# Mixing stage of a fused three-part kernel: where the next batch's value splits and the weight-rounding steps are issued

## The chip, the cores and the metric

The kernel runs on one core of one Trainium2 chip. The metric is the device time of one execution in microseconds (us). A core has TensorE (PE, matrix products), VectorE (DVE), ScalarE (ACT), GpSimd (POOL) and the queues that issue transfers, above all that of SyncE (SP). Each engine works through its own list of instructions in order; engines wait for each other through semaphores. On-chip data lies in SBUF (128 partitions), matrix products in the eight banks of PSUM.

## The reference

Three parts run one after the other. The change lies in the second, and in the preparation of the third's weights that runs beside it.

```python
# 1: delta-rule attention over (4, 8 heads, 768, 48), giving x of shape (4, 768, 384)
# 2:
h = gelu(x @ w_in)                       # (4, 768, 1024)
u, v = h[..., :512], h[..., 512:]
v_n = (v - mean(v)) / sqrt(var(v) + 1e-06) * g_ln
v_s = einsum('ts,bsd->btd', w_sg, v_n) + b_sg[None, :, None]     # the mixing over the 768 positions
x = x + (u * v_s) @ w_out                # gate, projection, addition
# 3:
k = relu(xk @ w_k); v = k * k @ w_v; r = sigmoid(xr @ w_r); out = r * v    # xk, xr: x mixed with its shift
```

All is float32. A product is made of three products of rounded parts: each operand is split into a high part `hi`, rounded to the format that PE multiplies fast, and a low part `lo = x - hi`, and `hi*hi + hi*lo + lo*hi` is summed (`mm3`, and `mix_mm` for the mixing).

## The kernel before, in words

The attention and the input projection come first; they leave the values v and the gates u in device memory (`vn_d`, `u_d`). The mixing follows, and after it the third part (ffn), in which PE is never without work for long.

**Halves.** The mixing runs over eight halves, `halves[k]` for k = 0 to 7, that is batch b = k // 2 and output half t = k % 2 (384 of the 768 positions). Below, h0 to h7. A half has four row blocks d (128 of the 512 channels). `mix(b, t, d)` multiplies the six chunks c of the batch's values with the half's mixing weights (18 matmuls into one PSUM bank), then gates on DVE: scale and bias out of PSUM (L897), multiplication with u (L899), and the split into `gh` (ACT, L108) and `gl` (DVE, L111). `project(b, t)` multiplies the four gated blocks with w_out (three groups of 12 matmuls, L139), each group followed by an addition into `xT` on DVE (L912 before, L911 in the changed kernel). For t = 0, `begin` first opens all four row blocks, so that PE does 48 matmuls (60 in h0) chunk by chunk. The projection of h(k-1) is put behind `begin` in an even half, behind the third row block in an odd one. PE's order is written out by hand (`manual_schedule`); the other engines' lists are made by a scheduler from the order of the program and its estimates.

**Values.** `load_v(b, c)` brings chunk c of batch b from device memory into `vst` (three buffers, L818, on SP's queue) and splits it into `vh` (ACT, L108) and `vl` (L111, 128x512) in a ring of nine; each of its chunks is read by both halves of its batch. The low part is made on GpSimd, for c = 0 and 3 on DVE. For the next batch three of the loads are issued ahead of the even half's last row block (`VF`), and all six splits behind the second row block of the odd half (`VD`).

**Weight roundings.** Beside all this the weights of the ffn are rounded and split by jobs (`narrow`): a load (L148, SP), six steps on DVE (L157, L159, L161, L163, L165, L167), an addition on POOL (L168), a rounding on ACT (L108), a subtraction on POOL (L111, `na<-na,raw`), and two stores (L196, SP). Steps on w_k are 128x256, on w_r and w_v 128x384. Two jobs are open at a time. `side(n)` issues the next n steps of the jobs; before the change it stands at three places: one step between the gate multiplication and the split, `SD` = 2 behind the split, and one behind each addition of a projection.

Of the kernel before, what the change touches and what calls it, by code (L numbers as in the profile page):

```python
# [16 lines left out]
B, H, S, D = 4, 8, 768, 48  # L17
# [32 lines left out]
NGL = 3  # L50
NNA = 2
PD = 2
SD = 2
CS = (5, 4)
VF = (0, 3)
VD = 1

E_LO_F = 2.0 ** -15
E_HI_F = 122879.9921875
# [15 lines left out]
def fused_kernel(  # L75
# [741 lines left out]
        vsts[b, c] = vr.tile([P, HF], F32, name="vst", bufs=3)  # L817
        nc.sync.dma_start(out=vsts[b, c], in_=vn_d[b, c])  # L818

    def load_v(b, c):  # L820
        if (b, c) not in vsts:
            fetch_v(b, c)
        to_ring(b, c, vsts.pop((b, c)))

    def to_ring(b, c, vst):
        vh = vr.tile([P, HF], F32R, name="vh")
        vl = vr.tile([P, HF], F32R, name="vl")
        split(A, G if c % 3 else V, vst, vh, vl)
        ring[b, c] = (vh, vl)

    ahead = [lambda i=i: load_ws(0, i) for i in range(6)]
# [55 lines left out]
    def mix(b, t, d):  # L887
        sl = slice(t * DM, t * DM + DM)
        pt, c0 = begun.pop(d, (None, 0))
        if pt is None:  # L890
            pt = ps.tile([P, HF], F32, name="ms")
        for c in range(c0, 6):
            mix_mm(pt, b, t, d, c)
        if d == 0:
            gs[b, t] = [mp.tile([P, 4, DM], F32R, name=x) for x in ("gh", "gl")]
        w = mp.tile([P, DM], F32, name="w")
        V.scalar_tensor_tensor(w, pt[:, :DM], g_sb[:, d:d + 1], b_sb[:, sl],  # L897
                               op0=ALU.mult, op1=ALU.add)
        V.tensor_tensor(w, w, us[b, t][:, d], op=ALU.mult)  # L899
        side(1)  # L900
        split(A, V, w, gs[b, t][0][:, d], gs[b, t][1][:, d])
        side(SD)

    def project(b, t):
        gh, gl = gs.pop((b, t))
        for f in range(3):
            pt = ps.tile([P, HF], F32, name="ms")
            fs = slice(f * P, f * P + P)
            mm3(pt[:, :DM], [((wo[0][:, c, fs], wo[1][:, c, fs]), (gh[:, c], gl[:, c]))
                             for c in range(4)])  # L910
            xs = xT[:, b, f, 1 + t * DM:1 + t * DM + DM]  # L911
            V.tensor_tensor(xs, xs, pt[:, :DM], op=ALU.add)  # L912
            side(1)

    load_u(0, 0)
    load_u(0, 1)
# [10 lines left out]
    for k, (b, t) in enumerate(halves):  # L927
# [6 lines left out]
        for d in range(4):  # L934
            if (t, d) == VF and b + 1 < B:
                for c in range(3):
                    fetch_v(b + 1, c)
            mix(b, t, d)
            if d == (PD if k < 7 else 3) and t:
                project(*halves[k - 1])  # L940
            if t == 1 and d == VD and b + 1 < B:
                for c in range(6):
                    load_v(b + 1, c)
        if k == 7:
            side(999)
        if k == 6:
# [123 lines left out]
```

## Time and profile before

| what | value |
|---|---|
| median of 3 runs | 811.81 us (810.57 to 814.44) |
| profiled execution, its own time | 811.44 us |
| its span in the trace | 809.7 us |
| granted TensorE clock, mean | 0.97 |
| PE busy | 747.1 us (92%) |
| DVE busy | 583.3 us (72%) |
| ACT busy | 344.3 us (43%) |
| POOL busy | 186.9 us (23%) |
| first matmul of the mixing to the end of its last projections | about 396 to 561 us |

How to read it: the shares are averages over three stages. The mixing is a fifth of the span; what an edit in it is worth is read from the places where PE waits there. Rows of a timeline give the start in us, the duration, the engine, the line of the program, what is written and read, and, in brackets, the idle time before the row and what ended it. "PEclk" is the granted clock, 1.00 being 2.4 GHz and 0.50 being 1.2 GHz.

### The profile page before, as it was taken

How to read it: one execution, taken by the hardware profiler on the slowest of the kernel's cores; microseconds unless marked ns; L12 is line 12 of the kernel's file. 1: busy time of each engine (PE TensorE's matmuls, PEld its weight loads, DVE VectorE, ACT ScalarE, POOL GpSimd, SP SyncE). 2: the span in 40 equal slices, each digit the busy share in tenths (PEclk: the TensorE clock that was granted, in tenths of full speed). 3: DMA queues.
4: the chain of work that ended last, by engine and by line, in shares of the span. 5: the costliest groups of instructions: out<-in, count | busy, mean ns of one | idle time of the engine just before them, and what ended most of it. 6: DMA issues, size and time to landing. Idle time of an engine off the chain costs nothing.

```text
span 809.7 us, 23901 instructions
## 1 busy us (share of the span) xinstructions
PE 747.1 (92%) x10206; PEld 656.5 (81%) x10206; DVE 583.3 (72%) x1253; ACT 344.3 (43%) x681; POOL 186.9 (23%) x197
## 2 busy tenths in 40 slices
PE   3368999999999998978989899899999999999998
PEld 3335667768778676767889799799999999999998
DVE  7989999689699698234779896988945655653442
ACT  2213454465555644634632231316744544542331
POOL 4125342232131323323324453340000000000000
PEclk9978999999999999989999889899999999999999
DMA  8403353354353443437987646449200000000000
GB/s 231 90 27 100 91 118 87 95 155 140 94 150 83 132 121 92 137 99 184 277 266 247 202 128 194 145 127 292 59 30 21 20 20 20 20 21 30 11 20 30
DMA packets 84970, 89.21 MB, mean 110 GB/s; under 512 B 25856, under 2 KB 68992, under 8 KB 84864
## 3 DMA queue, kind: packets, MB, share of 16 engines
q1 hardware_dynamic: 80128, 78.64, 32.8%
q0 software_dynamic: 4736, 9.04, 4.2%
q8 instruction: 80, 1.31, 0.7%
q14 instruction: 26, 0.21, 0.1%
HBM read 56.86 MB, written 26.08 MB: 102 GB/s over the span
## 4 chain that ended last, share of the span: by engine, by line
PE 60%; DVE 18%; DMA 7%; issue 6%; POOL 3%; ACT 2%; SPq 2%; DVEq 0%; POOLq 0%; ACTq 0%
PE ms L139 32%; PE ms L618 5%; PE ms L659 4%; PE rk L432 3%; PE ms L567 3%; PE ms L298 2%; DVE tmp L321 2%; PE ms L884 2%; DMA raw<-in_w_k_dram 2%; PE ms L502 2%; PE rk L468 2%; PE sps L488 2%; PE rk L444 2%; POOL na L168 1%; DVE na L157 1%
## 5 line engine op out<-in xcount | busy, mean ns | idle before, releaser
L168 POOL TENSOR_TENSOR na<-raw,na 128x256 f32<-128x256 f32 (+2 forms) x43 | 40.2, 938 | 149.7 <-DVE raw L167 110.0
L659 PE MATMUL ms<-warm 128*128 128x512 bf16 x222 | 62.1, 405 | 9.0 <-DVE warm L407 9.0
L139 PE MATMUL ms<-wvh,sh 128*128 128x384 f32 x192 | 64.9, 338 | 0.0
L139 PE MATMUL ms<-wvl,sh 128*128 128x384 f32 x192 | 64.9, 338 | 0.0
L139 PE MATMUL ms<-wvh,sl 128*128 128x384 f32 x192 | 64.8, 338 | 0.0
L139 PE MATMUL ms<-xm_hi,wkh 128*128 128x384 f32 x192 | 64.1, 334 | 0.0
L139 PE MATMUL ms<-xm_lo,wkh 128*128 128x384 f32 x192 | 64.1, 334 | 0.0
L139 PE MATMUL ms<-xm_hi,wkl 128*128 128x384 f32 x192 | 64.1, 334 | 0.0
L432 PEld LDWEIGHTS rk<-r,DT 32*32 32x32 f32 x1536 | 36.2, 107 | 28.7 <-DVE r L424 18.5
L111 DVE TENSOR_TENSOR sl<-r,sh 128x384 fp32r<-128x384 f32 x64 | 35.8, 559 | 30.3 <-ACT sh L108 30.3
L454 POOL TENSOR_SCALAR_AFFINE_SELECT SQ<-SQ 64x512 f32<-64x512 f32 x48 | 36.4, 759 | 86.6 <-ACT SQ L453 85.1
L432 PE MATMUL rk<-r,DT 32*32 32x48 f32 x1536 | 42.8, 205 | 13.0 <-DVE r L424 12.7
L424 DVE TENSOR_TENSOR r<-vk,rk 128x384 f32<-128x384 f32 x48 | 26.4, 549 | 38.4 <-PE rk L468 23.9
L108 ACT ACTIVATE sh<-r 128x384 fp32r<-128x384 f32 x64 | 33.6, 525 | 35.9 <-DVE r L990 35.9
L108 ACT ACTIVATE raw<-na 128x256 fp32r<-128x256 f32 (+2 forms) x31 | 13.7, 442 | 80.0 <-POOL na L168 78.1
L1006 DVE TENSOR_TENSOR ob<-th,ms 128x384 f32<-128x384 f32 x24 | 13.3, 553 | 43.3 <-PE ms L139 43.3
L300 PE MATMUL ms<-kT 64*32 64x64 f32 (+1 forms) x896 | 30.6, 225 | 13.9 <-issue 13.9
L618 PE MATMUL ms<-xh,wiu_hi 128*128 128x256 f32 x144 | 43.0, 298 | 0.0
L618 PE MATMUL ms<-xh,wiu_lo 128*128 128x256 f32 x144 | 42.9, 298 | 0.0
L618 PE MATMUL ms<-xl,wiu_hi 128*128 128x256 f32 x144 | 42.3, 294 | 0.6 <-issue 0.6
L990 DVE TENSOR_TENSOR r<-r 128x384 f32<-128x384 f32 x64 | 35.5, 554 | 9.6 <-ACT r L989 9.6
L157 DVE TENSOR_SCALAR na<-raw 128x256 uint32<-128x256 uint32 (+2 forms) x43 | 19.8, 461 | 30.1 <-DMA raw<-in_w_v_dram 7.7
(158 smaller groups left out, 2295.3 us busy)
## 6 DMA issues: line engine op xcount, KB each, us to landing
kT<-in_kt_d_dram SPq DMA_DIRECT2D x12, 512.0 KB, 4.5
u_d<-ug SPq DMA_DIRECT2D x48, 128.0 KB, 2.0
u<-u_d SPq DMA_DIRECT2D x8, 768.0 KB, 5.3
vn_d<-v SPq DMA_DIRECT2D x23, 256.0 KB, 3.9
vst<-vn_d SPq DMA_DIRECT2D x23, 256.0 KB, 3.4
SQ<-in_q_d_dram SPq DMA_DIRECT2D x48, 96.0 KB, 3.6
vk<-in_vk_dram SPq DMA_DIRECT2D x24, 192.0 KB, 3.9
vk<-in_vk_dram SPq DMA_DIRECT2D x12, 384.0 KB, 4.1
```

Of the source, the lines that this page charges most:

```text
L108: A.activation(hi, src, AF.Copy)
L111: eng_lo.tensor_tensor(lo, src, hi.bitcast(F32), op=ALU.subtract)
L139: T.matmul(pt, lhsT=a, rhs=b, start=(i == 0), stop=(i == n - 1))
L157: V.tensor_scalar(a, w_hi, 0x7FFFFFFF, None, op0=ALU.bitwise_and)
L168: G.tensor_tensor(af, f, af, op=ALU.add)
L300: T.matmul(gps[r + 32:r + 64, p, c0:c1], lhsT=t[r:r + 64, u, 32:64], rhs=vw2(t, r, 64, u * C + 32, [(0, (c1 - c0) // 32), (1, 32)]), start ...
L424: V.tensor_tensor(t, vt[s][:, 8 * o:8 * o + 8, :], RQs[o][:, :, 0:D], op=ALU.add)
L432: T.matmul(RQs[o][b0:b0 + 32, p, 0:D], lhsT=DT[b0:b0 + 32, u0 + p, :], rhs=t[b0:b0 + 32, p, :], start=True, stop=True, skip_group_check=True)
L454: G.affine_select(out=pt, in_=pt, pattern=[[0, 8], [1, C]], compare_op=ALU.is_gt, fill=0.0, base=0, channel_multiplier=-1)
L618: T.matmul(vstat["u"][:, 2 * P * d:2 * P * d + 2 * P], lhsT=w[:, c, ds_], rhs=a[:, c].rearrange("p b t -> p (b t)"), start=first, stop=last)
L659: T.matmul(o, lhsT=warm, rhs=vw(warm, 0, [(0, 4), (1, P)]), start=True, stop=True)
L990: V.tensor_tensor(r, r, r, op=ALU.mult)
```

## The change

The constants `SD` and `VD` give way to two tables, `ROW[t][d]` for the steps behind each row block and `ADD[t]` for those behind each addition. The step between the gate multiplication and the split is gone. In an even half one step follows each row block, in an odd half 2, 2, 1 and 8; each addition of the projection of an even half (which runs in an odd half) is followed by 5 steps, each of an odd half's by 2. An even half's calls then issue 10 steps (4, and 3 x 2 in the projection of the odd half before it), an odd half's 28 (13, and 3 x 5); before it was 15 in each (4 x 3, and 3 x 1). The splits of the next batch's values are issued one behind each row block of the odd half (chunks 0 to 2), chunk 3 ahead of the last row block's matmuls and 4 and 5 behind it; each load into `vst` of chunks 3 to 5 follows the split that frees its buffer. All these splits have their low part on GpSimd, none on DVE.

```diff
@@ -50,10 +50,10 @@
 NGL = 3
 NNA = 2
 PD = 2
-SD = 2
+ROW = ((1, 1, 1, 1), (2, 2, 1, 8))
+ADD = (5, 2)
 CS = (5, 4)
 VF = (0, 3)
-VD = 1
 
 E_LO_F = 2.0 ** -15
 E_HI_F = 122879.9921875
@@ -817,15 +817,15 @@
         vsts[b, c] = vr.tile([P, HF], F32, name="vst", bufs=3)
         nc.sync.dma_start(out=vsts[b, c], in_=vn_d[b, c])
 
-    def load_v(b, c):
+    def load_v(b, c, eng=None):
         if (b, c) not in vsts:
             fetch_v(b, c)
-        to_ring(b, c, vsts.pop((b, c)))
-
-    def to_ring(b, c, vst):
+        to_ring(b, c, vsts.pop((b, c)), eng)
+
+    def to_ring(b, c, vst, eng=None):
         vh = vr.tile([P, HF], F32R, name="vh")
         vl = vr.tile([P, HF], F32R, name="vl")
-        split(A, G if c % 3 else V, vst, vh, vl)
+        split(A, eng or (G if c % 3 else V), vst, vh, vl)
         ring[b, c] = (vh, vl)
 
     ahead = [lambda i=i: load_ws(0, i) for i in range(6)]
@@ -897,9 +897,8 @@
         V.scalar_tensor_tensor(w, pt[:, :DM], g_sb[:, d:d + 1], b_sb[:, sl],
                                op0=ALU.mult, op1=ALU.add)
         V.tensor_tensor(w, w, us[b, t][:, d], op=ALU.mult)
-        side(1)
         split(A, V, w, gs[b, t][0][:, d], gs[b, t][1][:, d])
-        side(SD)
+        side(ROW[t][d])
 
     def project(b, t):
         gh, gl = gs.pop((b, t))
@@ -910,7 +909,7 @@
                              for c in range(4)])
             xs = xT[:, b, f, 1 + t * DM:1 + t * DM + DM]
             V.tensor_tensor(xs, xs, pt[:, :DM], op=ALU.add)
-            side(1)
+            side(ADD[t])
 
     load_u(0, 0)
     load_u(0, 1)
@@ -935,12 +934,18 @@
             if (t, d) == VF and b + 1 < B:
                 for c in range(3):
                     fetch_v(b + 1, c)
+            nextv = t and b + 1 < B
+            if nextv and d == 3:
+                load_v(b + 1, 3, G)
             mix(b, t, d)
+            if nextv and d < 3:
+                load_v(b + 1, d, G)
+                fetch_v(b + 1, d + 3)
+            if nextv and d == 3:
+                load_v(b + 1, 4, G)
+                load_v(b + 1, 5, G)
             if d == (PD if k < 7 else 3) and t:
                 project(*halves[k - 1])
-            if t == 1 and d == VD and b + 1 < B:
-                for c in range(6):
-                    load_v(b + 1, c)
         if k == 7:
             side(999)
         if k == 6:
```

What the scheduler makes of it is seen in the order of the instructions. First DVE at the start of the gating, from the last mixing weights' splits (`ws1l`) to the first `gl` of h0; `raw` and `na` belong to one rounding job, a - stands only in the kernel before:

```order
 L111 TENSOR_TENSOR ws1l<-wst,ws1h 128x384 x5
 L897 SCALAR_TENSOR_TENSOR w<-ms,g_sb,b_sb 128x384 x2
-L157 TENSOR_SCALAR na<-raw 128x256
-L159 TENSOR_SCALAR na<-na 128x256
-L161 TENSOR_SCALAR na<-na 128x256
-L163 SCALAR_TENSOR_TENSOR na<-raw,na 128x256
-L165 TENSOR_SCALAR raw<-na 128x256
-L111 TENSOR_TENSOR vl<-vst,vh 128x512
-L167 SCALAR_TENSOR_TENSOR raw<-raw 128x256
 L899 TENSOR_TENSOR w<-w,u 128x384 x2
 L111 TENSOR_TENSOR gl<-w,gh 128x384 x2
```

One whole job and the split of batch 1's chunk 0 no longer stand ahead of the first gate multiplication.

Second, DVE between the last row block of h1 and the first addition of h1's projection. Before, from the last step of a w_k job on, ahead of the last `gl` of h1 (`na_7672` is a w_r job, 384 wide; `na_7246` a w_k job; `vl_7376` the split of a chunk of the next batch's values):

```order
L167 SCALAR_TENSOR_TENSOR raw_7041<-raw_7041 128x256
L157 TENSOR_SCALAR na_7672<-raw_7634 128x384
L111 TENSOR_TENSOR gl_6941<-w_7114,gh_6940 128x384
L159 TENSOR_SCALAR na_7672<-na_7672 128x384
L157 TENSOR_SCALAR na_7246<-raw_7121 128x256
L111 TENSOR_TENSOR vl_7376<-vst_7288,vh_7375 128x512
L159 TENSOR_SCALAR na_7246<-na_7246 128x256
L161 TENSOR_SCALAR na_7672<-na_7672 128x384
L161 TENSOR_SCALAR na_7246<-na_7246 128x256
L163 SCALAR_TENSOR_TENSOR na_7672<-raw_7634,na_7672 128x384
L163 SCALAR_TENSOR_TENSOR na_7246<-raw_7121,na_7246 128x256
```

In the changed kernel, from the last step of a w_r job on (`na_7639` is a second w_r job, `na_7117` and `na_7131` are w_k jobs):

```order
L167 SCALAR_TENSOR_TENSOR raw_7491<-raw_7491 128x384
L111 TENSOR_TENSOR gl_6924<-w_7106,gh_6923 128x384
L159 TENSOR_SCALAR na_7117<-na_7117 128x256
L157 TENSOR_SCALAR na_7639<-raw_7533 128x384
L161 TENSOR_SCALAR na_7117<-na_7117 128x256
L159 TENSOR_SCALAR na_7639<-na_7639 128x384
L163 SCALAR_TENSOR_TENSOR na_7117<-raw_7059,na_7117 128x256
L161 TENSOR_SCALAR na_7639<-na_7639 128x384
L165 TENSOR_SCALAR raw_7059<-na_7117 128x256
L157 TENSOR_SCALAR na_7131<-raw_7115 128x256
L167 SCALAR_TENSOR_TENSOR raw_7059<-raw_7059 128x256
```

Two w_r jobs stand in this stretch where there was one, and the split of a value chunk has left it.

Third, SP from the second three loads of batch 3's values (`vst`) to the w_v load (`raw`) that follows the stores of an earlier w_v job. Before:

```order
L818 DMA vst_7777<-vn_d_67 128x512
L818 DMA vst_7783<-vn_d_67 128x512
L818 DMA vst_7789<-vn_d_67 128x512
L196 DMA wr_dh_6779<-raw_7729 128x384
L196 DMA wr_dl_6780<-na_7823 128x384
L196 DMA wv_dh_6781<-raw_7821 128x384
L196 DMA wv_dl_6782<-na_7903 128x384
L148 DMA raw_7901<-in_w_v_dram 128x768
```

In the changed kernel:

```order
L818 DMA vst_7756<-vn_d_67 128x512
L818 DMA vst_7789<-vn_d_67 128x512
L818 DMA vst_7827<-vn_d_67 128x512
L196 DMA wv_dh_6781<-raw_7700 128x384
L196 DMA wv_dl_6782<-na_7821 128x384
L196 DMA wv_dh_6781<-raw_7819 128x384
L196 DMA wv_dl_6782<-na_7869 128x384
L148 DMA raw_7867<-in_w_v_dram 128x768
```

The stores ahead of the load are those of two w_v jobs now, where one of w_r and one of w_v were; the load still stands behind the three `vst` loads and four stores.

## Rows read from the trace of the kernel before

**Rows 1.** Windows: us; PE, PEld, DVE, ACT, POOL busy (instructions); clock; DMA; GB/s.

```profile
430.00:440.00 10.00, 10.00 (x60) 10.00 (x59) 9.83 (x19) 3.35 (x8) 5.37 (x6) 1.00 0.46 156
...
460.00:470.00 10.00, 8.56 (x20) 5.68 (x21) 9.38 (x24) 3.60 (x8) 2.11 (x4) 0.57 0.60 185
...
500.00:520.00 20.00, 16.66 (x73) 13.90 (x72) 19.15 (x38) 5.15 (x10) 7.42 (x6) 0.83 0.36 126
```

**Rows 2.** Timeline of PE in the mixing: first matmuls behind waits, last ahead of one.

```profile
418.80 0.44 PE L139 MATMUL ms<-gl,wo_hi 128*128 128x384 f32 x1 [0.48 <-DVE gl L111]
...
421.35 0.44 PE L139 MATMUL ms<-gh,wo_hi 128*128 128x384 f32 x1 [1.40 <-ACT gh L108]
...
458.15 0.34 PE L884 MATMUL ms<-ws1h,vl 128*128 128x384 f32 x1
...
460.94 0.44 PE L139 MATMUL ms<-gh,wo_hi 128*128 128x384 f32 x1 [2.45 <-ACT gh L108]
...
486.97 0.44 PE L139 MATMUL ms<-gl,wo_hi 128*128 128x384 f32 x1
...
510.32 0.69 PE L139 MATMUL ms<-gh,wo_hi 128*128 128x384 f32 x1 [1.70 <-ACT gh L108]
```

**Rows 3.** Timeline of DVE: the scale and bias of h2 d0, h3 d3 and h4 d0.

```profile
458.02 0.61 DVE L897 SCALAR_TENSOR_TENSOR w<-ms,g_sb,b_sb 128x384 f32<-128x384 f32 x1
...
482.34 0.61 DVE L897 SCALAR_TENSOR_TENSOR w<-ms,g_sb,b_sb 128x384 f32<-128x384 f32 x1
...
502.40 0.60 DVE L897 SCALAR_TENSOR_TENSOR w<-ms,g_sb,b_sb 128x384 f32<-128x384 f32 x1
```

**Rows 4.** Timeline of DVE: what a step and a value split take.

```profile
413.66 0.29 DVE L159 TENSOR_SCALAR na<-na 128x256 f32<-128x256 f32 x1
...
413.99 0.29 DVE L161 TENSOR_SCALAR na<-na 128x256 uint32<-128x256 uint32 x1
...
432.04 0.69 DVE L111 TENSOR_TENSOR vl<-vst,vh 128x512 fp32r<-128x512 f32 x1
...
467.20 0.29 DVE L165 TENSOR_SCALAR raw<-na 128x256 uint32<-128x256 uint32 x1
...
467.40 0.29 DVE L157 TENSOR_SCALAR na<-raw 128x256 uint32<-128x256 uint32 x1
...
476.00 0.35 DVE L165 TENSOR_SCALAR raw<-na 128x384 uint32<-128x384 uint32 x1
...
476.27 0.35 DVE L157 TENSOR_SCALAR na<-raw 128x384 uint32<-128x384 uint32 x1
```

**Rows 5.** Timelines of POOL and DVE: steps and a split beside POOL splits.

```profile
433.30 2.63 POOL L111 TENSOR_TENSOR vl<-vst,vh 128x512 fp32r<-128x512 f32 x2
...
434.82 1.26 DVE L161 TENSOR_SCALAR na<-na 128x256 uint32<-128x256 uint32 x1
...
481.13 1.28 DVE L111 TENSOR_TENSOR vl<-vst,vh 128x512 fp32r<-128x512 f32 x1
```

**Rows 6.** Timeline of DVE: first gate rows, first additions of the projections of h0, h1.

```profile
416.20 1.53 DVE L899 TENSOR_TENSOR w<-w,u 128x384 f32<-128x384 f32 x2 [0.19 <-DMA u<-u_d]
...
420.19 1.01 DVE L899 TENSOR_TENSOR w<-w,u 128x384 f32<-128x384 f32 x2
...
423.33 2.32 DVE L899 TENSOR_TENSOR w<-w,u 128x384 f32<-128x384 f32 x2
...
427.24 0.55 DVE L912 TENSOR_TENSOR xT<-xT,ms 128x384 f32<-128x384 f32 x1
...
450.97 0.55 DVE L912 TENSOR_TENSOR xT<-xT,ms 128x384 f32<-128x384 f32 x1
```

**Rows 7.** Timelines of POOL, SP and DVE around the w_v load (SPq: the issue).

```profile
491.40 1.03 POOL L168 TENSOR_TENSOR na<-raw,na 128x384 f32<-128x384 f32 x1 [0.89 <-DVE raw L167]
...
494.11 0.32 SPq L196 DMA_DIRECT2D wv_dl<-na  x1
...
497.79 0.36 DVE L157 TENSOR_SCALAR na<-raw 128x384 uint32<-128x384 uint32 x1 [6.00 <-DMA raw<-in_w_v_dram]
```

## The prediction, made before the changed kernel was run

> **What bounds the kernel now.** The windows come first: through the mixing DVE is busy 9 tenths of the time and more [rows 1], while PE loses time in two stretches above all, 460 to 470 (20 matmuls instead of 60, 0.57 of the clock granted) and 500 to 520 (73 instead of 120, 0.83 granted). Then the timeline of PE: from 396 to 561 us PE waits in the projections alone, for the gated blocks `gh` and `gl` [rows 2]. In the projection of h0 it waits 0.48 and 1.40 us; in that of h2 2.45, after which each next block comes in DVE's time; that of h3 starts nearly without a wait (486.97), that of h4 waits 1.70 in one place and goes in DVE's time. Third, the timeline of DVE says why. PE had the row blocks of h2 ready long before, but DVE gets to the first of them, L897, at 458.02 [rows 3], 0.13 us before PE comes to the end of the row blocks ahead of the projection (458.15). DVE works its list in order, and ahead of this row stand rounding steps. So what counts is how many rows stand in DVE's list ahead of three rows: h2 d0 (458.02), h3 d3 (482.34) and h4 d0 (502.40).
>
> **Prices.** Steps of 256 that don't wait for each other follow at 0.20 us (467.20 to 467.40), a step that needs the one ahead at 0.33 (413.66 to 413.99), steps of 384 at 0.27; for a dependent 384 step I add the same 0.13 and estimate 0.40 [rows 4]. A value split on DVE costs 0.60 (432.04, 0.69 with its overlap). A split on POOL takes 1.3 (2.63 for two), and beside it a DVE step took 1.26 instead of 0.29, so 0.97 more; a DVE split 1.28 [rows 5]. I price each POOL split that comes to lie beside steps at 0.97; the bounds are 0 (it lies beside rows out of PSUM or beside a wait) and 1.3 (its whole length).
>
> The Trainium skill, page "SBUF — State Buffer", section "SBUF: two separate sides", has a rule that speaks against this change: GpSimd and certain operations of DVE share a port pair under an exclusive lock, held for the whole instruction by whichever starts first, while the other fully blocks. By it the moved splits and all other POOL rows would cost DVE their whole length, and the time would be that of the slower rival below, 819.6 instead of 815.2; the row at 434.82 agrees in kind, at three quarters of the length.
>
> **Part 1, the start.** A job (six steps), one value split and the POOL rows of both no longer stand ahead of the first gate multiplication. That row waited for the transfer of u (0.19), so the steps themselves gain nothing; but the two L899 took 1.53 there, and an undisturbed pair 1.01; a later pair took 2.32 [rows 6]. Gain in the projection of h0: at least 0.5, at most the 1.88 that PE waits there; I take 0.9. DVE reaches the first addition of that projection (427.24) 0.9 + 0.7 = 1.6 earlier, the 0.7 being about half of the 1.31 that the later pair lost beside POOL splits, which are moved nearby, not removed.
>
> **Part 2, from the first addition of h0's projection (427.24) to that of h1's (450.97), 23.7 us.** Before, DVE has 25 steps of 256, 6 of 384 and 2 value splits there, after it 29, 12 and none, because the odd half now issues 28 steps and not 15. Steps: 4 x 0.20 + 6 x 0.27 = 2.4 if none depends, 4 x 0.33 + 6 x 0.40 = 3.7 if all do; two jobs interleave, so I take 2.8. Splits off DVE: 2 x 0.60 = -1.2. The same two splits beside the steps from POOL: 2 x 0.97 = +1.9. POOL's two rows of one more job, bounded by 0 and 1.3: +0.8. Sum +4.3; less the 1.6 of part 1, the first addition of h1's projection ends 2.7 later, at 450.97 + 0.55 + 2.7 = 454.2. **A new wait** hangs on this. All eight banks are taken there (four of h2, three of h1's projection, one of h3's first block), so the second row block of h3 waits for this addition. PE starts it 36 matmuls ahead of 458.15 [rows 2]; at 60 matmuls in 10 us [rows 1] that is 6.0 us earlier, 452.2, and before the bank was free at 451.5, 0.7 ahead. After, PE is there at 451.3 and waits till 454.2, 2.9 us: PE goes from 0.9 early to 2.0 late.
>
> **Part 3, up to h2 d0.** From that addition to L897 of h2 d0 DVE has 11 steps before and 8 after: -1.0 (3 x 0.33). L897 stands 2.7 - 1.0 = +1.7 late, and then the same number of steps stands between the blocks. So the projection of h2 ends about 1.8 later. This replaces the 2.0 of part 2, it is not added to it: PE arrives later and waits less.
>
> **Part 4, h3 d3.** From L897 of h3 d2 to that of d3 (482.34) there are 10 steps and a split (1.28, stretched) before, 14 steps and no split after, all near 0.40: +1.6 - 1.3; the split now made on POOL beside them +1.0. Together +1.3, so h3 d3 is 3.1 late. Nothing covers it: PE comes to the projection of h3 at 486.97 without idle time to give. That wait, now 1.3, is at once on the path: +3.1.
>
> **Part 5, h4.** DVE stands idle for 6.00 us until 497.79, for a w_v load [rows 7]. The load was issued behind a store at 494.11 that itself needs the POOL addition of 491.40 and the low part after it. In the new order of SP the load still stands behind three `vst` loads and four stores, so the chain moves with DVE: 3 to 4 us, I take 3.5 for L897 of h4 d0, and the rows from there to the last `gl` are as many as before. Queued behind the waiting step on DVE are the additions of h3's projection and then h4's gating.
>
> **Part 6, h5.** 13 steps against 14 and a split, with a POOL split more: -0.4 - 0.6 + 1.0 = 0; the 0.3 left is the split's stretch (1.28 less 0.97). The sum is 3.5 + 0.3 = +3.8, of which the parts are +1.8, +1.3, +0.4 and +0.3. The ffn has no slack and no gain.
>
> **The rivals.** *Faster: the w_v load comes loose.* The changed kernel is some ten steps further ahead in its jobs by h3, so a w_v load goes out earlier. If the load that bounds h4 is among those and lands ahead of 497, DVE's 6.0 idle shrinks to nothing and the projection of h4, which costs (120 - 73) / 120 x 20 = 7.8 us [rows 1], starts on time: 3.1 - 7.8 = -4.7, 806.7. Against it: the load has only two buffers and stands behind the stores in SP's list. *Same: the splits cost nothing.* If POOL's splits fall beside waits or rows out of PSUM, three times 0.97 goes, and the +3.8 becomes +0.9: 812.3. For it: L897 and L912 rows keep 0.55 to 0.61 throughout. *Slower: POOL keeps DVE out for all that it does.* If each added POOL row beside steps takes its whole length from DVE, part 2 pays two splits and the two rows of one more 384 job (1.03 for one at 491.40, [rows 7]): 2.6 + 2.1 = 4.7 instead of 2.7, and part 4 a split and two such rows, 1.3 + 2.1 = 3.4 instead of 1.0, so +4.4: 819.6. It decides from where POOL's rows start in the middle of a run of steps rather than beside L897 or L912. For it: 434.82 and 481.13 were stretched twofold and more. Against it: three quarters is what the row shows, and DVE was 9.83 of 10 us busy and PE without a wait where POOL was already 5.37 busy. *It doesn't do what it says*: the scheduler could put the steps back; the orders show it doesn't.
>
> **How the numbers follow.** The profiled execution took 811.44 (span 809.7 and 1.7 around it), 0.37 under the median. Forecast 811.44 + 3.8 = 815.2. 0.5% of 811.81 is 4.06 us, about what a measurement here can tell from no change: faster means below 807.75, slower above 815.87. The forecast's own range, from part 2's bounds (POOL prices 0 or 1.3, all steps dependent or none), is 812 to 818. Chances: forecast 0.50, of which 0.27 within 0.5% and 0.23 over; splits free 0.18 (within); POOL in full 0.13 (slower); load loose 0.19, of which 0.16 is faster and 0.03 within. Together faster 0.16, same 0.48, slower 0.36. The range 808.5 to 819 leaves out most of the faster case and half of the slower one, some 0.2.
>
> **What would show it.** Right: an idle time of 2 to 3 us ahead of h3's second row block, released by DVE L911; L897 of h2 d0 near 459.7 and of h3 d3 near 485.4; the projection of h3 starting with a wait of about 1.3; DVE idle for a w_v load near 500. Wrong: L911 of h1's projection at or ahead of 451 (steps and splits overpriced), no idle time on DVE around 495 (the load loose), or steps beside POOL rows stretched by more than 1.0 in most places.

## The result, and the profile after

The changed kernel is slower: 825.38 us (822.16 to 827.04, four runs) beside 813.12 us (810.57 to 815.81, four runs) of before, a ratio of 1.0146 (95% interval 1.0098 to 1.0193). In a second comparison on one chip it was 822.99 against 815.98 us, ratio 1.0087 (1.0063 to 1.0112). The forecast was 815.2, the range 808.5 to 819.0: the sign was right, the size too small, the time outside the range.

The first thing to settle is where the profiled execution loses its 14.2 us (span 823.9 against 809.7). The first matmul of the mixing (L884) stands at 396.05 before:

```profile
396.05 0.34 PE L884 MATMUL ms<-ws0h,vh 128*128 128x384 f32 x1
```

The same timeline of PE after: this first matmul, and then the first matmuls behind waits, as in [rows 2]:

```profile
403.12 0.34 PE L884 MATMUL ms<-ws0h,vh 128*128 128x384 f32 x1
...
427.74 0.44 PE L139 MATMUL ms<-gh,wo_hi 128*128 128x384 f32 x1 [1.39 <-ACT gh L108]
...
428.33 0.51 PE L139 MATMUL ms<-gl,wo_hi 128*128 128x384 f32 x1 [0.15 <-DVE gl L111]
...
463.36 0.69 PE L884 MATMUL ms<-ws1h,vh 128*128 128x384 f32 x1 [3.16 <-DVE xT L911]
...
474.14 0.44 PE L139 MATMUL ms<-gh,wo_hi 128*128 128x384 f32 x1 [0.41 <-ACT gh L108]
...
500.36 0.69 PE L139 MATMUL ms<-gl,wo_hi 128*128 128x384 f32 x1 [2.21 <-DVE gl L111]
...
523.95 0.54 PE L139 MATMUL ms<-gh,wo_hi 128*128 128x384 f32 x1 [1.24 <-ACT gh L108]
```

The mixing starts at 403.12, so 7.1 us are lost ahead of it, where PE has the same list in both kernels and the other engines nearly the same one; the granted clock differs there (0.90 before and 0.78 after in the first 100 us). From this matmul to the end it is 420.8 us against 413.7: +7.1, and that is the part which the prediction spoke of. Against the start of the mixing, the blocks end as follows (each is the start of the next block's first matmul):

| end of the projection of | before | after | change that arises there | forecast for it |
|---|---|---|---|---|
| h0 | 31.0 | 31.9 | +0.9 | -0.9 |
| h2 | 77.6 | 81.7 | +3.2 | +2.7 |
| h3 | 95.5 | 103.4 | +3.8 | +1.3 |
| h4 | 123.0 | 130.2 | -0.7 | +0.4 |
| h5 | 142.0 | 149.1 | -0.1 | +0.3 |
| sum | | | +7.1 | +3.8 |

The windows after, with the columns of [rows 1]:

```profile
430.00:440.00 10.00, 10.00 (x54) 10.00 (x53) 9.77 (x21) 3.56 (x7) 3.85 (x4) 0.90 0.79 281
...
440.00:450.00 10.00, 10.00 (x60) 10.00 (x59) 10.00 (x15) 2.51 (x5) 7.14 (x7) 1.00 0.62 195
...
450.00:460.00 10.00, 10.00 (x59) 9.88 (x57) 6.97 (x17) 1.36 (x3) 7.83 (x8) 1.00 0.30 103
...
460.00:470.00 10.00, 6.84 (x24) 6.64 (x23) 8.67 (x20) 1.46 (x3) 4.52 (x6) 0.66 0.74 235
...
500.00:510.00 10.00, 9.64 (x47) 9.64 (x48) 3.60 (x6) 1.16 (x2) 4.69 (x4) 0.83 0.68 228
```

DVE is at its limit from 430 to 450, but from 450 to 460 it is busy only 6.97 of 10 us, while POOL goes up from 3.85 to 7.83. The granted clock is below 1.00 in three of these windows, one of them (430 to 440) a window in which it was 1.00 before [rows 1]. The timeline of DVE after, with the rows that answer to [rows 3, 6, 7]: the first gate multiplication, the first additions of the projections of h0 (432.46) and h1 (462.76), the idle time ahead of the latter, L897 of h2 d0 (468.59) and of h3 d3 (494.71), and the step that waits for the w_v load:

```profile
423.36 1.03 DVE L899 TENSOR_TENSOR w<-w,u 128x384 f32<-128x384 f32 x2 [6.67 <-DMA u<-u_d]
...
432.46 0.54 DVE L911 TENSOR_TENSOR xT<-xT,ms 128x384 f32<-128x384 f32 x1
...
458.75 0.83 DVE L157 TENSOR_SCALAR na<-raw 128x256 uint32<-128x256 uint32 x1 [2.96 <-DMA wk_dl<-na]
...
462.76 0.55 DVE L911 TENSOR_TENSOR xT<-xT,ms 128x384 f32<-128x384 f32 x1
...
468.59 0.61 DVE L897 SCALAR_TENSOR_TENSOR w<-ms,g_sb,b_sb 128x384 f32<-128x384 f32 x1
...
494.71 0.60 DVE L897 SCALAR_TENSOR_TENSOR w<-ms,g_sb,b_sb 128x384 f32<-128x384 f32 x1
...
512.81 0.36 DVE L157 TENSOR_SCALAR na<-raw 128x384 uint32<-128x384 uint32 x1 [9.11 <-DMA raw<-in_w_v_dram]
```

Ahead of h1's first addition there is an idle time of 2.96 us that before does not have there. It ends when a store of a low part (`wk_dl<-na`) lands and frees the buffer `na` for the next step. The timeline of POOL, then of SP, shows where that store came from:

```profile
452.82 2.67 POOL L168 TENSOR_TENSOR na<-raw,na 128x256 f32<-128x256 f32 x1 [1.64 <-DVE raw L167]
...
456.03 0.73 POOL L111 TENSOR_TENSOR na<-na,raw 128x256 fp32r<-128x256 f32 x1 [0.53 <-ACT raw L108]
...
456.79 0.32 SPq L196 DMA_DIRECT2D wk_dl<-na  x1
```

The POOL addition at 452.82 took 2.67 us, the low part ended at 456.76, the store went out at 456.79, the step began at 458.75. POOL was not late with this addition: it had stood idle for 1.64 us ahead of it. The row was long while DVE ran short steps without a pause. Through this chain the bank of h3's second row block came free only at 463.3, and PE waited 3.16 us (463.36), where the prediction had 2.9.

The windows from the first addition of h0's projection to that of h1's, before and then after, part the growth of this stretch into rows and idle time of DVE (third busy time in a line):

```profile
427.24:450.97 23.73, 23.73 (x139) 23.73 (x138) 22.55 (x43) 6.43 (x12) 13.14 (x13) 1.00 0.61 206
...
432.46:462.76 30.30, 27.74 (x160) 27.42 (x158) 26.94 (x51) 7.12 (x14) 20.39 (x18) 1.00 0.55 178
```

Of the 6.6 us more, 4.4 are busy time of DVE and 2.2 idle time (1.18 before, 3.36 after).

### The profile page after: what moved, and what is told of

The parts are those of the page before. It is cut to its first block, busy times and chain, and to the rows that moved or that the text cites. A ratio compares the mean times of both kernels' runs of the same rounds, so it can differ in the third digit from the quotient of the medians.

```text
span 823.9 us, 23901 instructions
## 1 busy us (share of the span) xinstructions
PE 757.9 (92%) x10206; PEld 667.9 (81%) x10206; DVE 581.3 (71%) x1247; ACT 342.7 (42%) x681; POOL 194.6 (24%) x203
## 4 chain that ended last, share of the span: by engine, by line
PE 61%; DVE 18%; DMA 7%; issue 6%; POOL 4%; ACT 2%; SPq 2%; DVEq 0%; POOLq 0%; ACTq 0%
PE ms L139 31%; PE ms L618 5%; PE ms L659 5%; PE ms L567 4%; PE rk L432 4%; PE ms L298 2%; DVE tmp L321 2%; PE ms L884 2%; PE ms L502 2%; POOL na L168 2%; PE sps L488 2%; PE rk L468 2%; PE rk L444 2%; DVE na L157 1%; PE ms L300 1%
## 5 line engine op out<-in xcount | busy, mean ns | idle before, releaser
L432 PE MATMUL rk<-r,DT 32*32 32x48 f32 x1536 | 44.2, 209 | 13.6 <-DVE r L424 13.3
L108 ACT ACTIVATE sh<-r 128x384 fp32r<-128x384 f32 x64 | 33.5, 524 | 35.9 <-DVE r L995 35.9
L157 DVE TENSOR_SCALAR na<-raw 128x256 uint32<-128x256 uint32 (+2 forms) x43 | 21.1, 491 | 34.4 <-DMA wk_dl<-na 10.6
L659 PEld LDWEIGHTS <-warm 128*128 128x128 bf16 x222 | 18.4, 103 | 29.3 <-DVE warm L407 9.6
```

What stands on the lines that cost most here:

```text
L108: A.activation(hi, src, AF.Copy)
L157: V.tensor_scalar(a, w_hi, 0x7FFFFFFF, None, op0=ALU.bitwise_and)
L432: T.matmul(RQs[o][b0:b0 + 32, p, 0:D], lhsT=DT[b0:b0 + 32, u0 + p, :], rhs=t[b0:b0 + 32, p, :], start=True, stop=True, skip_group_check=True)
L659: T.matmul(o, lhsT=warm, rhs=vw(warm, 0, [(0, 4), (1, P)]), start=True, stop=True)
```

## The experiments

All times in this table are worked out from the timelines of PE and DVE of one profile each, against the first matmul of the mixing: where the blocks end, how long h3's projection lasts, the bank wait at h3's second row block (- if under 1 us), the stretch on DVE from the first addition of h0's projection to that of h1's, the landing of the w_v load that ends DVE's idle time ahead of h4, and the rest to the end of the span. The ratio is that of the timed runs.

| kernel | mixing starts | h0 ends | stretch | bank wait | h2 ends | h3 lasts | w_v lands | h4 ends | rest | ratio |
|---|---|---|---|---|---|---|---|---|---|---|
| before | 396.1 | 31.0 | 23.7 | - | 77.6 | 6.5 | 101.7 | 123.0 | 413.7 | 1 |
| before, again | 397.0 | 36.4 | 24.1 | - | 80.6 | 6.4 | 104.8 | 126.1 | 417.1 | 1 |
| after | 403.1 | 31.9 | 30.3 | 3.16 | 81.7 | 10.2 | 109.7 | 130.2 | 420.8 | 1.0146 |
| after, again (e1) | 400.9 | 33.1 | 30.3 | 3.21 | 81.6 | 11.2 | 110.3 | 131.5 | 421.5 | 1.0087 |
| steps only (e3) | 396.9 | 29.3 | 25.5 | - | 75.1 | 11.0 | 103.7 | 125.9 | 415.6 | 1.0016 |
| values only (e4) | 394.9 | 34.2 | 26.8 | 1.10 | 80.8 | 6.9 | 106.3 | 128.4 | 419.0 | 1.0060 |
| after, 2 splits on DVE (e5) | 400.3 | 30.1 | 27.0 | - | 76.5 | 12.2 | 105.9 | 127.1 | 417.8 | 1.0055 |
| before, splits on POOL (e6) | 398.9 | 34.4 | 26.3 | - | 79.3 | 6.9 | 105.4 | 127.0 | 417.8 | 1.0019 |
| after, three `na` (e7) | 398.1 | 32.3 | 29.1 | 2.71 | 81.7 | 6.9 | 108.0 | 128.8 | 419.3 | 1.0031 |
| after, 3 steps less at h3 (e8) | 399.3 | 33.0 | 30.3 | 3.21 | 81.7 | 8.1 | 109.9 | 129.7 | 421.1 | 1.0094 |
| after, 6 steps less at h1 (e9) | 398.5 | 31.1 | 28.4 | 1.28 | 80.6 | 12.4 | 107.2 | 126.7 | 418.8 | 1.0059 |
| after, loads by POOL (e11) | 398.7 | 33.5 | 31.4 | 4.31 | 80.2 | 14.2 | 107.4 | 131.1 | 427.9 | 1.0134 |
| steps only, three `na` (e12) | 400.8 | 30.9 | 27.9 | 2.44 | 81.1 | 6.3 | 105.2 | 126.0 | 416.4 | 0.9995 |
| e5 with three `na`, loads by POOL (e13) | 394.9 | 29.5 | 33.7 | 5.12 | 81.4 | 10.0 | 107.0 | 130.5 | 425.0 | 1.0102 |

**Both kernels once more (e1, e2), unchanged.** Is the part ahead of the mixing chance?

> The changed kernel once more. Its first profile ends 14.2 us later than that of before, but only 7.1 of them arise from the first matmul of the mixing on (before: 396.05 to 809.7, 413.7 us; changed: 403.12 to 823.9, 420.8 us); the other 7.1 lie ahead of it, where nearly all instructions are the same. Theory A (that part is chance of the single execution): the mixing starts within 2 us of 397 here, the part behind it takes 420 to 422 us, the time is 817 to 820 and the ratio about 1.009. Theory B (the change moves the earlier part too, by the loads and splits that are issued ahead of the mixing): the mixing starts at 402 to 404 again, the time is 824 to 827, the ratio 1.014 or more.

> The kernel before once more, for a second profile of it. Theory A: the start of the mixing scatters by some us, 394 to 402, and the part behind it is 413 to 415 us again. Theory B: the start lies at 396 within 1 us.

The ratio fell to 1.0087 and the rest was 421.5 us, as theory A had it; the time (822.99 us) and the start of the mixing (400.9) lay between the two theories. Before took 417.1 us from the mixing on in its second profile, 3.4 more than in the first and more than theory A allowed. It was 5.4 us late at the end of h0's projection, for whose gating the load of u landed at 23.1 and not at 20.2, and made up 2.4 of them by the end of h2's. Over all the profiles of the table the start of the mixing lies between 394.9 and 403.1. So the starts scatter, and so does the first projection. From the mixing on the changed kernel is 7.1 us slower in the first pair of profiles and 4.4 in the second. Whether a small part of the 7.1 ahead of the mixing belongs to the change as well stays open.

**Each half of the change alone (e3, e4).** e3 is before with the new tables and without `side(1)`; e4 is after with `side(1)`, `side(2)` and `side(1)` at the old places.

> Only the rounding steps are issued at the new places; loads and splits of the values as before, two of them per batch on VectorE. From the first addition of h0's projection to that of h1's VectorE then has 26 steps of 256, 12 of 384 and 2 splits (before 25, 6 and 2; changed kernel 29, 12 and 0). If the steps make the bank wait at h3's second row block (my theory), it is 2 to 3 us here and the part from the first mixing matmul on is 418 to 421 us. Rival (the splits on GpSimd make it, through the stretch of the steps beside them): no bank wait over 1 us, 413 to 416 us.

> Only the value splits move, one behind each row block and all on GpSimd; the rounding steps at the places of before. In the same stretch VectorE has 28 steps of 256, 6 of 384 and no split. My theory (the steps make the bank wait): wait under 1 us, the part from the first mixing matmul on 414 to 416 us, time within 2 us of before. Rival (the splits on GpSimd make it): a bank wait of 2 to 3 us, 418 to 421 us.

Neither theory holds by itself. The steps alone make no bank wait over 1 us, as the rival of e3 had it; the values alone make one of 1.10, between theory and rival, and their rest of 419.0 us is the rival's; only together they make 3.2. In the stretch on DVE the steps alone add 1.6 us to the 23.9 of before (mean of two), the values alone 2.9, both 6.4. The total goes the same way, 1.0016 and 1.0060 against 1.0087, but the first cannot be told from no change (0.9999 to 1.0034). But h3's projection is late from the steps alone. In e3, L897 of h3 d2 and d3 (here L898) and PE's wait that follows:

```profile
471.91 0.61 DVE L898 SCALAR_TENSOR_TENSOR w<-ms,g_sb,b_sb 128x384 f32<-128x384 f32 x1
...
485.64 0.60 DVE L898 SCALAR_TENSOR_TENSOR w<-ms,g_sb,b_sb 128x384 f32<-128x384 f32 x1
...
488.35 0.45 PE L140 MATMUL ms<-gh,wo_hi 128*128 128x384 f32 x1 [1.93 <-ACT gh L109]
```

15 steps and a split stand between the two row blocks, 13.7 us; before it was 10 and a split, 10.4 us.

**Engine or place of the splits (e5, e6).**

```diff
 # e5, against the changed kernel
-load_v(b + 1, d, G)
+load_v(b + 1, d)          # likewise chunks 3 to 5: chunks 0 and 3 on VectorE again
 # e6, against the kernel before
-split(A, G if c % 3 else V, vst, vh, vl)
+split(A, G if (b or c % 3) else V, vst, vh, vl)
```

> The changed kernel, but the low parts of chunks 0 and 3 of each next batch are made on VectorE as before; all issue places stay new. VectorE has 26 steps of 256, 12 of 384 and 2 splits from the first addition of h0's projection to that of h1's, as with the new step places alone. Theory P (the splits moved to GpSimd fill that engine until the rounding jobs wait for their `na` buffers: VectorE idle 2.96 us ahead of h1's first addition, in both profiles of the changed kernel): that idle time is gone, the stretch takes 25 to 26 us and not 30.3, h3's second row block waits under 1 us, the part from the first mixing matmul on is 415 to 417.5 us and the ratio 1.001 to 1.004. Rival I (the issue places of the splits, not their engine): all as in the changed kernel, 420 to 422 us.

> The kernel before with nothing changed but the engine: all splits of the next batch's values on GpSimd, issue places as before. VectorE's list is that of before less the six splits. Theory P: VectorE loses to the stretch of its steps as much as or more than the 0.6 us a split gave back; from the first addition of h0's projection to that of h1's 25 to 27 us (before 23.7 and 24.1), ratio 1.003 to 1.006. Rival I: the places did it, so this is the same as before or up to 1.5 us faster, the stretch 22.5 to 23.5 us.

In e6 DVE's list is that of before less two splits in the stretch, 1.2 us of its own work, and yet the stretch grows by 2.4 us, as theory P had it. The ratio of 1.0019 (0.9997 to 1.0041), 1.003 to 1.006 expected, cannot be told from no change. The timeline of DVE in e6, from the first addition of h0's projection to that of h1's (457.22):

```profile
430.93 0.55 DVE L912 TENSOR_TENSOR xT<-xT,ms 128x384 f32<-128x384 f32 x1
...
454.40 0.43 DVE L167 SCALAR_TENSOR_TENSOR raw<-raw 128x256 f32<-128x256 uint32 x1
...
457.01 0.29 DVE L157 TENSOR_SCALAR na<-raw 128x256 uint32<-128x256 uint32 x1 [2.18 <-POOL na L111]
...
457.22 0.55 DVE L912 TENSOR_TENSOR xT<-xT,ms 128x384 f32<-128x384 f32 x1
```

The window of the stretch in e6, to be read beside the 22.55 us of DVE above:

```profile
430.93:457.22 26.29, 26.29 (x153) 26.29 (x153) 23.06 (x41) 6.63 (x13) 16.54 (x16) 1.00 0.62 200
```

DVE is busy 0.5 us longer than before (22.55 and 22.61 us in its two profiles), though 1.2 us of splits are gone: its other rows take 1.7 us more beside POOL's, 0.85 for each moved split. The other 1.9 us are idle time (3.23 against 1.18 and 1.53), most of it the 2.18 at 457.01. The profile puts this wait down to POOL's low part. But that row belongs to another job than the step, by the program's buffer numbers. The step reads `raw_7280`, whose w_k load landed at 456.88 by its semaphore, 0.13 us ahead of the step; the landing of the `wk_dl` store in the changed kernel (458.62) stands as far ahead of the step at 458.75. The issue of this load by SP, in before and then in e6:

```profile
444.34 0.33 SPq L148 DMA_DIRECT2D raw<-in_w_k_dram  x1
...
453.22 0.38 SPq L148 DMA_DIRECT2D raw<-in_w_k_dram  x1
```

In before it stands ahead of the two stores of `raw_7121` and `na_7246` in SP's list (447.38 and 448.71). In e6 the scheduler has put it behind them, and the second of them waits for a low part of POOL. So e6 is not a change of the engine alone. It shows what a moved split costs beside DVE's steps, 0.85 us, and apart from that what the place of one load in SP's list is worth.

The other way round, e5 takes the splits back and loses the bank wait and, but for 0.29 us, the 2.96 of idle time: with the new places kept, the splits on POOL are what brings both. Its stretch of 27.0 is above the 25 to 26 expected. The total stays at 1.0055 (1.001 to 1.004 expected); h3's projection takes 12.2 us, with 15 steps and a split ahead of h3 d3 as in e3.

**A third `na` buffer (e7).** `NNA = 3`, and two buffers for the loads of w_sg in place of three.

> The changed kernel with three buffers `na` for the 128x256 rounding jobs where there are two (the space comes from the buffers of the mixing weights' loads, two and not three). VectorE's list moves a little: 30 steps of 256 and 12 of 384 in the same stretch (changed kernel 29 and 12). If the two buffers cause the idle time of 2.96 us, it is gone, h1's first addition comes 2 to 3 us earlier against the start of the mixing, and the bank wait falls from 3.2 to under 1.5 us; if GpSimd's speed causes it, the idle time only moves behind other steps and the stretch still takes 29 to 31 us.

The idle time of 2.96 is gone, but the stretch still takes 29.1 us, in 28.0 of which DVE is busy (26.9 in the changed kernel), and PE still waits:

```profile
458.58 0.44 PE L884 MATMUL ms<-ws1h,vh 128*128 128x384 f32 x1 [2.71 <-DVE xT L911]
```

So the buffers were where a part of the delay showed: without that wait the steps run beside POOL's rows and are stretched. For the stretch that is the second of the two outcomes put down; the bank wait fell, but to 2.71 and not under 1.5. By-products: with two buffers for w_sg, PE waits 1.94 us for a mixing weight in h0; and the order moved, 10 steps stand between h3 d2 and d3, and h3's projection lasts 6.9 us.

**Rows taken out at one place (e8, e9).** In `narrow`, under a condition on the job, the second to fourth step are left out: for the first w_v job (e8), for the first two w_r jobs (e9).

> The changed kernel, with the first w_v job leaving out three of its six VectorE steps (the middle ones, so its part of w_v is not rounded as it should be). VectorE's list is that of the changed kernel but for these three rows, and they stand between the scale and bias of h3 d2 and of h3 d3: 11 steps there and not 14 (before 10). Theory C (the number of rows there sets what h3's projection loses: 6.4 to 6.9 us long with 9 or 10 steps, 10.2 to 12.2 with 14 or 15, in nine profiles so far): the projection takes 6.5 to 8 us, the bank wait at h3's second row block stays at about 3.2, the part from the first mixing matmul on is 417 to 418.5 us. Rival: the projection is late because all that comes before it is late: still 10 us or more, 420 to 422 us.

> The changed kernel, with the first two w_r jobs leaving out three of their six VectorE steps each (their part of w_r is not rounded as it should be). From the first addition of h0's projection to that of h1's 29 steps of 256 and 6 of 384 are left (changed kernel 29 and 12), the list around h3 d3 is unchanged. If the bank wait hangs on the rows of VectorE there, it falls from 3.2 to under 1 us, the end of h2's projection comes 2.5 to 4 us earlier (77.5 to 79.5 us from the first mixing matmul, not 81.7), and h3's projection still takes 10 us or more; the part from the first mixing matmul on is 416.5 to 418.5 us. Rival (GpSimd, not VectorE's rows, sets that stretch): it still takes 29 to 30 us, the wait stays over 2 us.

e8, DVE (L898 is the scale and bias): three rows less bring h3 d3 from 11.9 to 8.6 us behind h3 d2, and h3's projection falls to 8.1 us, just over the 6.5 to 8 of theory C.

```profile
480.23 0.60 DVE L898 SCALAR_TENSOR_TENSOR w<-ms,g_sb,b_sb 128x384 f32<-128x384 f32 x1
...
488.82 0.61 DVE L898 SCALAR_TENSOR_TENSOR w<-ms,g_sb,b_sb 128x384 f32<-128x384 f32 x1
...
493.02 1.28 DVE L157 TENSOR_SCALAR na<-raw 128x384 uint32<-128x384 uint32 x1 [2.58 <-DMA raw<-in_w_v_dram]
...
509.26 0.36 DVE L157 TENSOR_SCALAR na<-raw 128x384 uint32<-128x384 uint32 x1 [8.92 <-DMA raw<-in_w_v_dram]
```

The total does not fall (421.1 us, the rival's number): the wait for the w_v load at 509.26 lasts 8.92 us and ends at 109.9 against the mixing's start, just where it ends in the changed kernel (109.7 and 110.3). What is won at h3 is lost again at h4. e9 takes six rows of 384 out of the stretch, which falls by 1.9 us, and the bank wait by 1.9:

```profile
457.63 0.44 PE L885 MATMUL ms<-ws1h,vh 128*128 128x384 f32 x1 [1.28 <-DVE xT L912]
```

That is over the 1 us expected. The rest falls by 2 to 3 us, which is less than the 3.4 by which the two profiles of before differ. What the stretch loses is idle time, from 3.4 to 3.8 us (changed kernel, e1, e8) to 1.7; DVE is busy as long as with the six rows (26.7 us against 26.6 to 26.9), since the rows that are left take longer beside POOL's. Of the 4.5 us that remain over the 23.9 of before, four more steps of 256 (0.9) and two splits less (-1.2) explain nothing: it is the length of the rows, not their number, that is left.

**The queue of SP (e11).** In the changed kernel the w_v load that bounds h4 stands behind loads that wait for POOL. POOL, then SP:

```profile
497.43 1.12 POOL L111 TENSOR_TENSOR na<-na,raw 128x384 fp32r<-128x384 f32 x1
...
504.31 1.29 POOL L111 TENSOR_TENSOR vl<-vst,vh 128x512 fp32r<-128x512 f32 x1
...
499.92 6.03 SPq L818 DMA_DIRECT2D vst<-vn_d  x3
...
505.99 0.42 SPq L196 DMA_DIRECT2D wv_dh<-raw  x1
...
509.04 0.33 SPq L148 DMA_DIRECT2D raw<-in_w_v_dram  x1
```

The low part of the first w_v job ends at 498.55, but the job's first store goes out at 505.99, behind three `vst` loads that hold the queue for 6.03 us until POOL's split of 504.31 has freed the last buffer; the w_v load, which needs the buffer that this store reads, follows at 509.04, as the store has landed. e11 puts these loads on POOL's queue:

```diff
-nc.sync.dma_start(out=vsts[b, c], in_=vn_d[b, c])
+(G if b and c >= 3 else nc.sync).dma_start(out=vsts[b, c], in_=vn_d[b, c])
```

> The changed kernel, with the loads of chunks 3 to 5 of each next batch issued from GpSimd's queue and not from SP's. In the changed kernel these loads hold SP (6.03 us for three at 499.92) until GpSimd's splits free their buffers; the stores of the first w_v job, whose low part was ready at 498.55, go out behind them at 505.99, and the w_v load that needs that buffer goes out at 509.04 and ends an idle time of 9.11 us on VectorE at 512.81. In eleven profiles the end of h4's projection lies 19.5 to 22.2 us behind that landing. Theory S (the loads that wait for GpSimd's splits hold up the w_v load on SP): the load lands 5 us or more earlier against the first mixing matmul (104 to 105, not 110), h4's projection ends at 125 to 128 and not 130 to 131.5, the part from the first mixing matmul on is 416 to 419 us though h3's projection stays late. Rival: the load is late because its job is late on VectorE, GpSimd's longer list makes it later still: landing 109 to 112, 420 to 423 us.

The issue of the w_v load, DVE's waits for w_v loads, and PE's rows from h4's start to the end of h4's projection:

```profile
499.93 0.33 SPq L148 DMA_DIRECT2D raw<-in_w_v_dram  x1
...
506.13 0.36 DVE L157 TENSOR_SCALAR na<-raw 128x384 uint32<-128x384 uint32 x1 [3.27 <-DMA raw<-in_w_v_dram]
...
511.09 0.75 DVE L157 TENSOR_SCALAR na<-raw 128x384 uint32<-128x384 uint32 x1 [1.76 <-DMA raw<-in_w_v_dram]
...
490.68 0.45 PE L884 MATMUL ms<-ws0h,vh 128*128 128x384 f32 x1 [2.24 <-ACT vh L108]
...
502.92 0.69 PE L139 MATMUL ms<-gl,wo_hi 128*128 128x384 f32 x1 [3.70 <-DVE gl L111]
...
523.57 0.33 PE L139 MATMUL ms<-gh,wo_hi 128*128 128x384 f32 x1
...
529.63 0.34 PE L139 MATMUL ms<-gh,wo_lo 128*128 128x384 f32 x1
```

The load goes out 4.7 us earlier against the start of the mixing (101.2 and not 105.9), so the hold on SP is real. But it takes 6.1 us to land and not 3.6, and lands at 107.4, between theory S (104 to 105) and its rival (109 to 112); a second wait of 1.76 follows. The end of h4's projection (131.1) and the rest (427.9) miss the ranges of theory S. That this projection runs without a wait, 523.57 to 529.63 (36 matmuls in 6.2 us, against 13.3 in the changed kernel), does not show that the load was its bound, as it also begins 7.9 us later, when the gated blocks are ready. The ratio is worse, 1.0134: the values of h4 come late (2.24 at 490.68), the bank wait grows to 4.31, and `gl` of h3 is 3.70 late (502.92). That the load issues in POOL's list make POOL later and so do this is likely, but not tested by itself.

**In search of a version that beats both (e12, e13).** e12 is e3, e13 is e5 with the loads of e11, both with the buffers of e7.

> The new step places with values as before (two splits per batch on VectorE) and three `na` buffers, two for the loads of the mixing weights. VectorE's list has 31 steps of 256, 12 of 384 and 2 splits from the first addition of h0's projection to that of h1's (new step places alone 26, 12, 2; changed kernel 29, 12, 0), but only 10 steps and a split between h3 d2 and h3 d3 (new step places alone 15 and one). Theory C: h3's projection takes 6.4 to 7.5 us (11.0 with the new step places alone); the stretch ahead takes 26 to 28 us and brings a bank wait of 0 to 1.5 us; the part from the first mixing matmul on is 412 to 415 us, ratio 0.994 to 0.999. Rival: the bank wait eats it, 416 to 419 us, ratio 1.001 or more.

> The changed kernel with chunks 0 and 3 split on VectorE, the loads of chunks 3 to 5 on GpSimd's queue, and three `na` buffers. VectorE's list has 33 steps of 256, 12 of 384 and 2 splits in the first stretch, 11 steps and a split between h3 d2 and h3 d3, and 6 steps and not 9 ahead of h4. If the terms found add up, a bank wait of 1 to 2.5 us comes, h3's projection takes 6.5 to 8 us, and h4's takes less than 10 (13.3 to 13.7 in both kernels): 411 to 415 us from the first mixing matmul on, ratio 0.992 to 0.999. Rival (GpSimd's list, longer by nine load issues, delays all): ratio 1.002 or more.

e12 confirms the count at h3: 10 steps and a split, 9.8 us, and a projection of 6.3 us. But a stretch of 27.9 us brings a bank wait of 2.44, over the 0 to 1.5 expected, and the ratio is 0.9995 (0.9968 to 1.0022): no gain. PE, then DVE:

```profile
460.06 0.69 PE L885 MATMUL ms<-ws1h,vh 128*128 128x384 f32 x1 [2.44 <-DVE xT L912]
...
480.56 0.61 DVE L898 SCALAR_TENSOR_TENSOR w<-ms,g_sb,b_sb 128x384 f32<-128x384 f32 x1
...
490.36 0.60 DVE L898 SCALAR_TENSOR_TENSOR w<-ms,g_sb,b_sb 128x384 f32<-128x384 f32 x1
```

In e13 the terms do not add up, the rival came: 1.0102. Its stretch takes 33.7 us, PE waits 5.12 us for the bank, and h3's projection takes 10.0 us with 11 steps and a split ahead of h3 d3, so the count alone does not set it. 8.4 us of the stretch are idle time of DVE. POOL, then DVE:

```profile
440.16 5.84 POOL L111 TENSOR_TENSOR vl<-vst,vh 128x512 fp32r<-128x512 f32 x1 [3.10 <-DMA raw<-in_w_k_dram]
...
451.61 0.99 DVE L157 TENSOR_SCALAR na<-raw 128x256 uint32<-128x256 uint32 x1 [6.76 <-issue]
```

A POOL split that takes 1.3 to 1.9 us elsewhere takes 5.84 here, beside short steps of DVE without a pause, and ends 1.15 us after the last of them. The rounding rows behind it, the stores and a w_k load on SP come so much later, and DVE's next step reads what that load brings. A further table of steps (e10) gives no time: it leaves a third of `wk_dl` unwritten. No version that beats before was found.

## Why the prediction was too small, step by step

**What bounds the kernel** held for two of the three rows named (L897 of h2 d0 and of h3 d3): +3.2 and +3.8 us arise at the projections behind them. L897 of h4 d0 comes 7.2 us later than before where 3.5 were forecast, but PE comes as late, and nothing arises there (-0.7).

**Two steps failed: the idle time of DVE in part 2 and the clock behind the new wait in part 4. Both were put at nothing.**

**Prices.** A split that moves to POOL was priced at 0.97 us, what a step beside it loses by [rows 5], with 1.3 as the upper bound. e6 measured 0.85 for each, so this price was right, and so was the sum of the rows in part 2: +4.3 forecast, +4.4 busy time of DVE measured. What the sum left out is the way of a buffer `na`, from the last step of a rounding job on DVE (ending at 452.74) through an addition on POOL, a rounding on ACT and a low part on POOL to the landing of the store (458.62). It takes 5.9 us, and DVE had only 3.0 us of other steps meanwhile; what is left is the 2.96 us of idle time. Such a wait cannot simply be taken off again: with a third buffer (e7) it is gone, and DVE is busy 1.1 us longer. The slower rival, "POOL keeps DVE out for all that it does" (819.6, chance 0.13), comes near in the stretch, 6.3 against 6.6, but by luck: it had no idle time and priced the rows too high. It rests on the rule of the Trainium skill, "SBUF — State Buffer", "SBUF: two separate sides". That rule, a lock held for a whole instruction, agrees in kind with rows that are longer beside POOL's, and 0.85 is less than the whole 1.3; the waits through buffers lie beyond it.

**Part 1** was right on DVE, whose first addition of h0's projection comes 1.9 us earlier (29.3 against 31.2 behind the first matmul; 1.6 forecast), and had the wrong sign on PE in the pair of profiles: h0's projection ends 0.9 later, not 0.9 earlier. The first gate multiplication waits for u in both, 20.2 us behind the first matmul, and in the changed kernel DVE stands idle for 6.67 us ahead of it. PE's wait was shorter (1.39 and 0.15 against 0.48, 1.40 and 0.15), but afterwards the granted clock was 0.90 from 430 to 440, where before it was 1.00 all through this projection. That sign is chance of the pair: in all ten profiles with new step places the projection ends at 29.3 to 33.5, on average 31.5, in the four with the old ones at 31.0 to 36.4, on average 34.0.

**Part 2** was right in its mechanism: the bank wait came at h3's second row block. That its size fits, 3.16 us against 2.9, is luck. The addition that frees the bank came 4.7 us later than before and not 2.7, by the idle time; PE, forecast 0.9 early, came 0.9 late. The two errors cancel. The steps were sized well: e3 has seven more and takes 1.6 us more, some 0.23 each.

**Part 3** took L897 of h2 d0 as +1.7; it is 65.5 against 62.0 behind the first matmul, +3.5. All of the difference comes from part 2.

**Part 4** was right about DVE and wrong about PE. From h3 d2 to d3 the changed kernel takes 11.9 us against 10.4, +1.5 where +1.3 was forecast. But the wait that follows was 2.21 us, not 1.3, and the projection 3.8 us longer: the row at 500.36 lasts 0.69 instead of 0.33 to 0.45 and the clock of 500 to 510 is 0.83, which makes 1.7 us of these ten. The prediction named the lower clock only where before already showed it (0.57 from 460 to 470, [rows 1], with the wait of 2.45 us in [rows 2]) and put it at nothing behind the waits that it forecast. The same holds at 463.36 (0.69, and 0.66 granted from 460 to 470). That the rows ahead of h3 d3 set this loss is shown by e8 and e12, where fewer rows bring h3's projection to 8.1 and 6.3 us.

**Part 5** was right that DVE would stand idle for a w_v load, but the reason was another. The idle time grew from 6.00 to 9.11 because the store and the load stood behind `vst` loads that wait for POOL. The load landed 8.0 us later (109.7 against 101.7) where 3.5 were forecast. The prediction saw those three `vst` loads in SP's order and gave them no cost of their own. Since PE came 7 us later as well, h4's projection lost no more than before (13.3 us against 13.7). In e8 this load lands as late as in the changed kernel, and what is won at h3 does not reach the end; whether an earlier load alone would bring it there stays open, as e11 moved other waits too.

**The range** was missed above all by what the prediction did not speak of: of the 10.5 us between 815.2 and the profiled execution (825.66), 3.3 arise in the mixing (+7.1 against +3.8) and 7.1 ahead of it. It was worked out around 811.81 without the scatter of the runs. The median of before was 813.12 with one more run, and 813.8 to 816.1 in the later comparisons; forecast in the ratio, 815.2 was +0.4%, and +0.9% to +1.5% was measured.

## What to carry to other kernels

Work that is moved to an engine which stands in the middle of a pipeline can cost more than the time in which the two overlap: the first engine's next steps need buffers that come back through the second. Before moving it, follow one buffer round, with the second engine's rows and the store on the way (5.9 us here), and compare it with the work that the first engine has meanwhile (3.0 us).

In an engine's or a queue's list, count what stands ahead of the row on which the slow engine waits, and look for entries that themselves wait: three loads that wait for a buffer held up a store by 7 us, and the load behind it, though they had nothing to do with them. Ask, too, whether the engine that a profile names as releaser holds what the row reads: in e6 it named POOL, and the row read what a load had brought.

When a wait is removed, the next one on the same path must be priced before the gain is booked: here bank, `gl`, and w_v load took turns.

## What the runs showed that was not expected

With the same list on PE up to the mixing, its start lay between 394.9 and 403.1 us in fourteen profiles, and two executions of the kernel before differed by 3.4 us from there on; one load of u landed 3.0 us later in the second.

A POOL addition of 128x256, 0.74 to 0.99 us in most rows, took 2.67 us at 452.82, and in e13 a POOL split 5.84 us at 440.16, 1.3 to 1.9 in the others; in both places DVE ran short steps without a pause. So the loss between the two engines goes both ways.
